# Emitting five engine streams straight into the main program, without a Block around them

## The chip, the cores and the metric

One core of one Trainium2 chip. The metric is the device time of one execution in microseconds (us).

The *span* is what the profile shows, from the start of the first instruction to the end of the last one of this program. The *time* is the metric; it is longer than the span (245.03 against 243.30 us in the profiled run of the kernel before). *Time minus span*: 1.73 us, though no instruction of the kernel lies in it. A store *lands*, as the word is used here, at the last count that the trace records for the semaphore of its transfer, a counter that an engine's instruction can wait for.

## The reference

A diffusion transformer block on x of 2 x 256 x 1152 in bf16, weights in bf16:

```python
B, N, D, F, H = 2, 256, 1152, 4608, 2
shift_a, scale_a, gate_a, shift_m, scale_m, gate_m = (silu(c) @ w_mod).reshape(B, 6, 1, D)   # split on axis 1
h = layernorm(x) * (1 + scale_a) + shift_a
q, k, v = h @ wqkv                                    # two heads of 576
a = softmax(q k^T * 576**-0.5) v @ wo
x = x + gate_a * a
h2 = layernorm(x) * (1 + scale_m) + shift_m
return x + gate_m * (gelu(h2 @ w_fc1) @ w_fc2)
```

## The kernel before

The kernel keeps a list of operations for each of the five engines (PE, ACT, DVE, POOL and SP, which issues 71 of the 79 transfers). A scheduler in Python works out their order and the semaphore waits. `emit` then writes each list into the program. Only `emit` and the line that opens the Block are touched by the change.

```python
outs = [ins for u in order["sp"] for ins in u.instrs if ins.is_out]     # 14 stores of the result
last_out = outs[-1]

def run_engine(e, eng_handle):
    for u in order[e]:
        for ins in u.instrs:
            if ins is last_out:                       # wait for all stores but the last four
                for o in outs[:-4]:
                    eng_handle.wait_ge(dma_sems[o.dma_sem], o.dma_val)
            for (k, v) in waits[ins.gidx]:
                # ... wait_ge on a DMA's semaphore or on an engine's
            bi = ins.fn(eng_handle)
            # ... bi.then_inc(...)
    if e == "sp":                                     # SP waits until the result is stored
        for o in outs[-4:-1]:
            eng_handle.wait_ge(dma_sems[o.dma_sem], o.dma_val)
        eng_handle.wait_ge(dma_sems[last_out.dma_sem], last_out.dma_val)

block.sync(lambda eng: run_engine("sp", eng))
block.tensor(lambda eng: run_engine("pe", eng))
# ... scalar, vector, gpsimd the same

# in build_kernel:
with (
    nc.sbuf_tensor("arena", ...) as arena,
    nc.psum_tensor("psum", ...) as psum,
    nc.Block() as block,                              # line 554
):
```

A Block gives each engine a body of its own. The author expected of it a branch into each body, a branch from the body to the Block's end, and a barrier of all engines there. Of the branches, the trace shows SP's at the end alone (38 ns at 242.919 us). The barrier is in the trace: the DRAINs of SP, ACT, DVE and PE count one semaphore (96) up; POOL's wait for it starts at 243.121 us, 25 ns after the last of them, SP's, has ended; POOL counts a second one (97) up at 243.199, and the waits of the other four for it start at 243.240 to 243.253. SP alone waits for the stores to land. The others have nothing to do after their last operation.

Of the kernel before, what the change touches and what calls it, by code (L numbers as in the profile page):

```python
# [171 lines left out]
class Sched:  # L172
# [222 lines left out]
        for e in ENGINES:  # L395
            print(e, "%.1f" % (sum(u.end - u.start for u in self.order[e]) / 1000))

    def emit(self, nc, block, sems, dma_sems):
        order = self.order
        eidx = {e: 0 for e in ENGINES}  # L400
        dma_cnt = [0] * len(dma_sems)
        n_other = getattr(self, "n_other_dma_sems", 8)
        n_sp = len(dma_sems) - n_other
        di = 0
        dj = 0
        for e in ENGINES:
            for u in order[e]:
                for ins in u.instrs:
                    if u.dma_bytes > 0:
                        if e == "sp":  # L410
                            k = di % n_sp
                            di += 1
                        else:
                            k = n_sp + dj % n_other
                            dj += 1
                        dma_cnt[k] += 16
                        ins.dma_sem = k
                        ins.dma_val = dma_cnt[k]
                    else:
                        eidx[e] += 1  # L420
                        ins.eidx = eidx[e]
        self.final_counts = dict(eidx)
        self.final_dma = list(dma_cnt)
        snap = {}
        stats = {"waits": 0}

        def sem_of(d):
            if d.dma_sem is not None:
                return ("d", d.dma_sem), d.dma_val
            return ("e", d.unit.eng), d.eidx  # L430

        allu = sorted(self.units, key=lambda u: (u.start, u.uid))
        known = {e: {} for e in ENGINES}
        waits = {}
        for u in allu:
            e = u.eng
            kn = known[e]
            for ins in u.instrs:
                need = {}
                for d in ins.deps:  # L440
                    k, v = sem_of(d)
                    if need.get(k, 0) < v:
                        need[k] = v
                wl = []
                for k, v in sorted(need.items(), key=lambda kv: (-kv[1], str(kv[0]))):
                    if kn.get(k, 0) >= v:
                        continue
                    wl.append((k, v))
                    kn[k] = v
                    for d in ins.deps:  # L450
                        if sem_of(d) == (k, v):
                            sn = snap.get(d.gidx)
                            if sn:
                                for kk, vv in sn.items():
                                    if kn.get(kk, 0) < vv:
                                        kn[kk] = vv
                            break
                waits[ins.gidx] = wl
                stats["waits"] += len(wl)
                snap[ins.gidx] = dict(kn)  # L460
        self.wait_stats = stats

        outs = [ins for u in order["sp"] for ins in u.instrs if ins.is_out]
# [5 lines that stand above are left out]
                    if ins is last_out:  # L469
# [3 lines that stand above are left out]
                        if k[0] == "d":  # L473
                            eng_handle.wait_ge(dma_sems[k[1]], v)
                        else:
                            eng_handle.wait_ge(sems[k[1]], v)  # L476
                    bi = ins.fn(eng_handle)
                    if ins.dma_sem is not None:
                        bi.then_inc(dma_sems[ins.dma_sem], 16)
                    else:  # L480
                        bi.then_inc(sems[e], 1)
            if e == "sp":
                for o in outs[-4:-1]:
                    eng_handle.wait_ge(dma_sems[o.dma_sem], o.dma_val)
                eng_handle.wait_ge(dma_sems[last_out.dma_sem], last_out.dma_val)

        block.sync(lambda eng: run_engine("sp", eng))
        block.tensor(lambda eng: run_engine("pe", eng))
        block.scalar(lambda eng: run_engine("act", eng))
        block.vector(lambda eng: run_engine("dve", eng))  # L490
        block.gpsimd(lambda eng: run_engine("pool", eng))



# [50 lines left out]
def build_kernel(nc, x, c, wqkv, wo, w_mod, w_fc1, w_fc2, out):  # L545
    S = Sched()
# [4 lines left out]
    with (  # L551
        nc.sbuf_tensor("arena", [P, ARENA_BYTES // 2], BF16) as arena,
        nc.psum_tensor("psum", [P, 4096], F32) as psum,
        nc.Block() as block,
    ):
        def sb(off, nbytes, dt=BF16):
            assert off % 4 == 0 and off + nbytes <= ARENA_BYTES, (off, nbytes)
# [741 lines left out]
        with ExitStack() as es:  # L1299
            sems = {e: es.enter_context(nc.semaphore("c_" + e)) for e in ENGINES}  # L1300
            dma_sems = [es.enter_context(nc.semaphore("d%d" % i)) for i in range(56)]
            S.emit(nc, block, sems, dma_sems)
    return S


# [3 lines left out]
def bass_standalone__dit_block__diffusion_kernel(  # L1309
    nc: bass.Bass,  # L1310
    x: bass.AP,
    c: bass.AP,
    wqkv: bass.AP,
    wo: bass.AP,
    w_mod: bass.AP,
    w_fc1: bass.AP,
    w_fc2: bass.AP,
    out: bass.AP,
):
    build_kernel(nc, x, c, wqkv, wo, w_mod, w_fc1, w_fc2, out)  # L1320
# [28 lines left out]
```

## Time and profile before

| | before |
|---|---|
| time, median of 6 runs (range) | 245.33 us (245.23 to 245.52) |
| time / span of the profiled run | 245.03 / 243.30 us |
| PE busy | 238.9 us, 98% of the span |
| last matmul ends / last store landed / last instruction ends | 240.59 / 242.81 / 243.30 us |

These lines of the page of the kernel before give the span, the engines' busy time, the granted clock in 40 slices (9 is 90% or more), and the shares of the chain of work that ended last.

```profile
span 243.3 us, 4087 instructions
...
PE 238.9 (98%) x1763; PEld 148.1 (61%) x1763; DVE 120.4 (49%) x217; ACT 67.2 (28%) x136; POOL 21.4 (9%) x39
...
PEclk9999999999999999999999999999999999999999
...
PE 94%; ACT 2%; DMA 2%; DVE 1%; POOL 0%; issue 0%; DVEq 0%
```

The kernel is bound by its matmuls (PE is 94% of the chain). A change that does not touch them can only win at the ends. The end of the chain in order of time (start us, us, what), kernel before:

```profile
105.90 134.88 PE psum L692 x848
240.78 0.02 issue
240.80 0.24 DVE arena L1272
241.04 0.02 issue
241.06 0.22 DVE arena L1273
```

The chain of work ends at 241.28 us, but the span ends at 243.3. The two microseconds in between hold no work of an engine: they are the last store on its way and then the closing of the Block. The instructions of line 554, the `with` that holds the Block, show the latter (engine, operation, count: durations in ns, first and last start in us; the letter q marks instructions of the engine's sequencer, which the page does not count as busy time):

```profile
L554 POOLq EVENT_SEMAPHORE  x2: 17/17/17, 243.1 to 243.2; - x2
L554 POOLq DRAIN  x1: 4317/4317/4317, 162.8 to 162.8; - x1
L554 ACTq DRAIN  x1: 626/626/626, 170.2 to 170.2; - x1
L554 PEldq DRAIN  x1: 897/897/897, 239.9 to 239.9; - x1
L554 DVEq DRAIN  x1: 261/261/261, 241.1 to 241.1; - x1
L554 SPq COMPARE_BRANCH  x1: 38/38/38, 242.9 to 242.9; - x1
L554 SPq DRAIN  x1: 7/7/7, 243.1 to 243.1; - x1
L554 SPq EVENT_SEMAPHORE  x1: 17/17/17, 243.2 to 243.2; - x1
L554 ACTq EVENT_SEMAPHORE  x1: 17/17/17, 243.2 to 243.2; - x1
L554 DVEq EVENT_SEMAPHORE  x1: 21/21/21, 243.3 to 243.3; - x1
L554 PEldq EVENT_SEMAPHORE  x1: 51/51/51, 243.3 to 243.3; - x1
```

Read it by the starts. The four DRAINs at 162.8 to 241.1 us come before the last store has landed (242.81), so they cost nothing, not even POOL's of 4.3 us. SP's branch, SP's DRAIN and all the semaphore instructions come after it and are exposed.

The start of the kernel before, in order of time (start us, us, engine, line, operation, out<-in, count):

```profile
0.80 0.84 SPq L673 DMA_DIRECT2D arena<-in_x_dram  x2
...
1.42 1.28 ACT L730 ACT_TABLE_LOAD   x1 [1.42 <-PEq L1334]
```

### The profile page before, as it was taken

How to read it: one execution, taken by the hardware profiler on the slowest of the kernel's cores; microseconds unless marked ns; L12 is line 12 of the kernel's file. 1: busy time of each engine (PE TensorE's matmuls, PEld its weight loads, DVE VectorE, ACT ScalarE, POOL GpSimd, SP SyncE). 2: the span in 40 equal slices, each digit the busy share in tenths (PEclk: the TensorE clock that was granted, in tenths of full speed). 3: DMA queues.
4: the chain of work that ended last, by engine and by line, in shares of the span. 5: the costliest groups of instructions: out<-in, count | busy, mean ns of one | idle time of the engine just before them, and what ended most of it. 6: DMA issues, size and time to landing. Idle time of an engine off the chain costs nothing.

```text
span 243.3 us, 4087 instructions
## 1 busy us (share of the span) xinstructions
PE 238.9 (98%) x1763; PEld 148.1 (61%) x1763; DVE 120.4 (49%) x217; ACT 67.2 (28%) x136; POOL 21.4 (9%) x39
## 2 busy tenths in 40 slices
PE   7999999999999999999999999999999999999995
PEld 2698854556667666898444444444565666656575
DVE  3824378596997799789999500000022221111112
ACT  4830350345424207973233222223000000000000
POOL 1500000000021186400000000020000000000000
PEclk9999999999999999999999999999999999999999
DMA  7999999999995999989953498002000000000000
GB/s 233 332 379 393 390 390 391 396 414 405 392 354 183 341 396 392 392 268 394 316 160 84 150 320 310 0 21 80 0 16 19 16 16 19 16 16 22 29 16 19
DMA packets 30140, 51.59 MB, mean 212 GB/s; under 512 B 1703, under 2 KB 15787, under 8 KB 30123
## 3 DMA queue, kind: packets, MB, share of 16 engines
q1 hardware_dynamic: 29680, 50.14, 57.9%
q0 software_dynamic: 416, 1.19, 1.7%
q8 instruction: 14, 0.23, 0.4%
q14 instruction: 3, 0.02, 0.0%
q10 hardware_dynamic: 27, 0.00, 0.0%
HBM read 50.14 MB, written 1.19 MB: 211 GB/s over the span
## 4 chain that ended last, share of the span: by engine, by line
PE 94%; ACT 2%; DMA 2%; DVE 1%; POOL 0%; issue 0%; DVEq 0%
PE psum L692 93%; PE psum L695 2%; DMA arena<-in_x_dram 2%; ACT arena L753 1%; ACT arena L751 1%; DVE arena L764 0%; POOL arena L755 0%; DVE arena L1272 0%; DVE arena L1273 0%; DVE arena L754 0%; DVE arena L746 0%; DVEq L476 0%
## 5 line engine op out<-in xcount | busy, mean ns | idle before, releaser
L692 PE MATMUL psum<-arena 128*128 128x384 bf16 (+10 forms) x1674 | 235.7, 307 | 1.5 <-POOL arena L715 1.5
L692 PEld LDWEIGHTS psum<-arena 128*128 128x128 bf16 (+3 forms) x1674 | 142.9, 97 | 90.1 <-issue 4.5
L1067 DVE SCALAR_TENSOR_TENSOR arena<-arena 128x1152 f32<-128x1152 bf16 x32 | 44.7, 1414 | 0.6
L1272 DVE TENSOR_TENSOR arena<-psum,arena 128x384 f32<-128x384 f32 (+3 forms) x14 | 7.0, 501 | 68.0 <-PE psum L692 68.0
L1181 ACT ACTIVATE arena<-psum 128x512 bf16<-128x512 f32 (+1 forms) x44 | 22.4, 520 | 42.7 <-PE psum L692 42.7
L687 ACT ACTIVATE arena<-psum 128x512 bf16<-128x512 f32 (+6 forms) x37 | 19.6, 550 | 38.7 <-PE psum L692 37.0
L689 DVE CAST arena<-psum 128x512 bf16<-128x512 f32 (+3 forms) x13 | 8.2, 641 | 11.4 <-PE psum L692 11.3
L673 POOL DMA_DIRECT2D dit_scratch<-arena x3 | 1.8, 616 | 115.3 <-DVE arena L689 58.5
L1149 POOL TENSOR_TENSOR arena<-arena 128x384 f32<-128x384 f32 x12 | 10.9, 912 | 10.8 <-DVE arena L1148 9.4
L1094 DVE CAST arena<-psum 72x32 bf16<-72x32 f32 x1 | 0.2, 188 | 21.3 <-PE psum L692 21.3
L743 DVE BATCH_NORM_STATS2 arena<-arena 128x6 f32<-128x384 f32 (+1 forms) x18 | 9.6, 551 | 0.3
L1154 ACT ACTIVATE arena<-arena 128x1152 bf16<-128x1152 f32 x4 | 5.3, 1344 | 11.8 <-DVE arena L1153 11.8
L1273 DVE TENSOR_TENSOR arena<-arena 128x384 bf16<-128x384 f32 (+3 forms) x14 | 7.0, 501 | 0.5
L1148 DVE TENSOR_TENSOR arena<-psum,arena 128x384 f32<-128x384 f32 x12 | 6.5, 547 | 1.5 <-PE psum L692 1.4
L695 PE MATMUL psum<-arena 128*128 128x128 bf16 (+1 forms) x89 | 7.1, 219 | 0.2 <-DVE arena L764 0.2
L695 PEld LDWEIGHTS psum<-arena 128*128 128x128 bf16 (+1 forms) x89 | 5.8, 98 | 2.2 <-DMA arena<-in_c_dram 0.8
L1168 DVE TENSOR_SCALAR arena<-psum,arena 128x128 bf16<-128x128 bf16 x20 | 5.4, 334 | 1.9 <-PE psum L695 1.9
L1171 ACT ACTIVATE arena<-psum,arena 128x128 bf16<-128x128 bf16 x16 | 6.0, 456 | 1.0 <-PE psum L692 0.6
L1074 DVE TENSOR_REDUCE arena<-arena 128x36 f32<-128x1152 f32 x4 | 5.4, 1345 | 0.0
L1071 DVE STREAM_TRANSPOSE arena<-arena 128x1152 f32<-128x1152 f32 x4 | 5.4, 1362 | 0.0
L997 ACT ACTIVATE arena<-psum,arena 128x256 bf16<-128x256 f32 x8 | 3.7, 472 | 1.3 <-PE psum L692 0.9
L951 ACT ACTIVATE arena<-arena 128x256 bf16<-128x256 bf16 x6 | 2.6, 498 | 3.9 <-DVE arena L945 3.9
(48 smaller groups left out, 45.9 us busy)
## 6 DMA issues: line engine op xcount, KB each, us to landing
arena<-in_w_fc_dram SPq DMA_DIRECT2D x9, 1152.0 KB, 7.1
arena<-in_w_fc_dram SPq DMA_DIRECT2D x4, 2592.0 KB, 17.3
arena<-in_wqkv_dram SPq DMA_DIRECT2D x18, 288.0 KB, 10.4
arena<-in_w_mod_dram SPq DMA_DIRECT2D x3, 1728.0 KB, 20.3
arena<-in_w_mod_dram SPq DMA_DIRECT2D x3, 864.0 KB, 13.4
arena<-in_w_mod_dram SPq DMA_DIRECT2D x9, 288.0 KB, 10.7
arena<-in_wqkv_dram SPq DMA_DIRECT2D x1, 2592.0 KB, 16.7
arena<-in_wo_dram SPq DMA_DIRECT2D x1, 2592.0 KB, 24.4
```

What stands on the lines that cost most here:

```text
L687: act(c_act(n), lambda e: e.activation(out=dst, in_=src, func=ACTF.Copy), [src], [dst], name)
L689: dve(c_dve_psum16(n) if psum16 else c_dve_psum32(n), lambda e: e.tensor_copy(dst, src), [src], [dst], name)
L692: S.instr(lambda e: e.matmul(o, lhsT=l, rhs=r, start=st, stop=sp, **kw), reads=[l, r], writes=[o])
L695: S.instr(lambda e: e.transpose(o, i_, idn), reads=[i_, idn], writes=[o])
L743: dve(550, lambda e, s=s, o=o: e.bn_stats(out=o, in_=s), [s], [o], "bn_%s_%d" % (tag, ci))
L1067: dve(1270, lambda e, w=w, s=s, acc=acc: e.scalar_tensor_tensor(out=acc, in0=w, scalar=s, in1=acc, op0=ALU.mult, op1=ALU.add), [w, s, acc] ...
L1148: dve(550, lambda e, o=o, ga=ga, x1c=x1c: e.tensor_tensor(out=x1c, in0=o, in1=ga, op=ALU.mult), [o, ga], [x1c], "wo_t1_%d_%d" % (t, ci))
L1149: S.op("pool", 930, lambda e, xs=xs, x1c=x1c: e.tensor_tensor(out=x1c, in0=x1c, in1=xs, op=ALU.add), reads=[x1c, xs], writes=[x1c], name=" ...
L1171: act(440, lambda e, o=o, dst=dst, s1=s1, s2=s2: e.activation(out=dst, in_=o, func=ACTF.Identity, scale=s1, bias=s2), [o, s1, s2], [dst], ...
L1181: act(c_act(ntok), lambda e: e.activation(out=dst, in_=o, func=ACTF.Gelu_apprx_tanh), [o], [dst], "gelu_%d_%d" % (f, tok0))
L1272: dve(c_dve_psum32(w), lambda e, o=o, gm=gm, t1=t1: e.tensor_tensor(out=t1, in0=o, in1=gm, op=ALU.mult), [o, gm], [t1], "fc2_t1_%d_%d" % ( ...
L1273: dve(c_dve_32(w), lambda e, t1=t1, x1c=x1c, ost=ost: e.tensor_tensor(out=ost, in0=t1, in1=x1c, op=ALU.add), [t1, x1c], [ost], "fc2_out_%d ...
```

## The change

The intent is to save what the Block adds: the branches and the closing barrier. The same lists are written into the one main program, each instruction with its engine's handle.

```diff
-    def emit(self, nc, block, sems, dma_sems):
+    def emit(self, nc, sems, dma_sems):
 ...
-        block.sync(lambda eng: run_engine("sp", eng))
-        block.tensor(lambda eng: run_engine("pe", eng))
-        block.scalar(lambda eng: run_engine("act", eng))
-        block.vector(lambda eng: run_engine("dve", eng))
-        block.gpsimd(lambda eng: run_engine("pool", eng))
+        for e, eng in (("sp", nc.sync), ("pe", nc.tensor), ("act", nc.scalar), ("dve", nc.vector), ("pool", nc.gpsimd)):
+            run_engine(e, eng)
 ...
         nc.psum_tensor("psum", [P, 4096], F32) as psum,
-        nc.Block() as block,
     ):
 ...
-            S.emit(nc, block, sems, dma_sems)
+            S.emit(nc, sems, dma_sems)
```

## The prediction

> **What bounds the kernel now.** TensorE. The page's busy table gives PE 238.9 us of a 243.3 us span (98%), and the chain of waits is PE for 94%: from 11.3 to 240.8 us it is matmuls and transposes, with the granted clock at full in all 40 slices. What is not PE lies at the ends: 11.3 us before the first dependent transpose (loading x 3.96 us, layernorm statistics), and 2.5 us after the last matmul (two DVE operations of 0.24 and 0.22 us, the last 16 KB store, 1.4 us to landing, then the Block's end).
>
> **What the change removes, adds, moves.** Work per engine, order, semaphores and buffers stay: the same scheduler fills the same lists, only the emission differs. The Block stands for:
> 1. A branch into each engine's body. The instruction records show none executed: after the opening barrier (the library's own, it stays) SP is released at 0.71 us and issues its first DMA 83 ns later, as between another SP wait and its DMA (81 ns near the end). Nothing is won at the start.
> 2. A branch from each body to the Block's end. Only SP's is in the records (it carries the last store wait): 38 ns at 242.92 us; SP's next instruction, a DRAIN, starts at 243.09, 170 ns after the branch did.
> 3. The closing barrier (line of the `with`): SP DRAIN 243.09, POOL's semaphore instructions 243.12 and 243.20, release of the others 243.24 to 243.30. The other engines' DRAINs run earlier and are hidden (PE 239.9, DVE 241.1 us).
> Added: one plain wait on SP for the one that the branch carried.
>
> **How much is critical.** Items 2 and 3 come after the last store landed (242.81 us), so they are exposed: from about 242.94 to 243.30, 0.35 us. [...] After the span the runtime has its own barrier[...]. The profiled run's time (245.03) is 1.73 us above the span, so part of it may be counted. Four engines will now wait there before SP arrives, so it may shorten: one hop of it comes 213 ns after the one before, where the same hop takes 38 ns in the preamble; 0 to 0.25 us may be saved. The 239 us of matmuls are untouched.
>
> **Predicted time.** 245.29 - 0.35 - about 0.10 = 244.85 us (estimate), range 244.45 to 245.25. Faster by over 2%: 0.01; within 2%: 0.98; slower: 0.01. Repeats differ by 0.3 us, so it is just visible.
>
> **What would show each step.** Span 242.9 to 243.0 us. No DRAIN, branch or barrier semaphore after the last store wait; SP's wait is the last instruction. Start unchanged: first DMA about 80 ns after SP's release, dependent transposes at 11.3 us. PE busy within 0.3 us of 238.9, same matmul count. Time minus span 1.5 to 1.75 us.
>
> **What would make it wrong.** The library closing the main program with a barrier of its own (then no gain); other placing of waits or of the activation table load (1.28 us at 1.42 us on ACT, hidden now behind loading x) when all engines share one block; shifted instruction fetches starving PE (its 16 KB fetches take about 1.1 us each, hidden now); noise as large as the effect.

245.29 (median of the three runs known then) - 0.35 - 0.10 comes to 244.84, and the forecast says 244.85. The 0.35 us were read from the trace. The 0.10 us, and that a part of the 1.73 us above the span is the runtime's barrier, were estimates. What the trace of before shows beside them is two rows of nine counts of one semaphore, described below, and in them one step (from the second to the third) of 213 ns after the kernel and 38 ns ahead of it.

## More of the kernel before

All runs but one are fast ones (granted TensorE clock 0.998 to 1.000); the one slow run is named where it occurs and is used for no time.

PE is the engine that is released last (its semaphore instruction lasts 51 ns and ends the span).

The wait for the last store is the instruction ahead of the branch:

```profile
L485 SPq EVENT_SEMAPHORE  x1: 28/28/28, 242.8 to 242.8; - x1
```

In the trace it starts at 242.829 us, 16 ns after the landing. The branch (242.919 us) also carries a wait on a store, but on an older one, which had landed at 237.40 us; so the branch waits for nothing.

## The result, and the profile after

Ratios are the mean time of one kernel's fast runs over that of the other's fast runs of the same rounds, so not quite the ratio of the medians.

| | before | after |
|---|---|---|
| time, median of 6 runs (range) | 245.33 us (245.23 to 245.52) | 244.28 us (243.99 to 244.74) |
| ratio, 95% interval | | 0.9958 (0.9946 to 0.9971) |
| time / span of the profiled run | 245.03 / 243.30 us | 244.28 / 243.00 us |
| time minus span | 1.73 us | 1.28 us |
| last store landed | 242.81 us | 242.85 us |

The change is a win of about 1 us (0.4%). It is clear of the noise, and larger than predicted: 244.28 lies below the low end of the range, 244.45. The table already shows where to look: the span fell by 0.3 us, and time minus span by 0.45 us, though no instruction of the kernel lies there.

The page of the changed kernel, the same lines:

```profile
span 243.0 us, 4065 instructions
...
PE 238.2 (98%) x1753; PEld 148.0 (61%) x1763; DVE 120.4 (50%) x217; ACT 67.2 (28%) x136; POOL 21.5 (9%) x39
...
PE 94%; DMA 3%; SPq 1%; issue 0%; DVE 0%
```

The 22 instructions fewer are the Block's 12, and 10 matmuls whose records are missing from this trace (the weight loads are all there, 1763 of 1763, and so are the compiled matmuls). The chain's shares at the start differ because it is followed back through another of two inputs: in after through the transfer of w_mod, which ends at 10.75 us, in before through layernorm's DVE operation, which ends at 11.28 us (11.05 in after).

The start and the end of the changed kernel's run, in order of time; first the start:

```profile
0.79 0.84 SPq L669 DMA_DIRECT2D arena<-in_x_dram  x2
...
1.43 1.28 ACT L726 ACT_TABLE_LOAD   x1 [1.43 <-PEq L1330]
```

Nothing moved there: the records show no branch at the start of either kernel. The first dependent transposes came at 11.1 instead of 11.3 us, but by 14.3 us the two runs are level again. The end of its chain:

```profile
169.43 71.39 PE psum L688 x507
240.84 0.24 DVE arena L1268
241.07 0.02 issue
241.10 0.23 DVE arena L1269
```

The last piece of work starts 0.04 us later than before, so the matmuls gave nothing. Line 554's instructions are gone; the last instruction of the program is now SP's wait for the last store (line 485):

```profile
L485 SPq EVENT_SEMAPHORE  x1: 28/28/28, 243.0 to 243.0; - x1
```

What lies after the span can be seen from the trace's records of semaphore 2. No instruction of the kernel touches it and it stands on no page. It is taken here for the counter of a barrier of the runtime; that is inferred, since a row of nine counts, from -0.370 to 0.001 us in before, also leads up to the start of the span. All that follows about this barrier is read from these counts. Each count is called a mark here. The nine marks of the first barrier after the kernel's work, in us from the start of the span:

```
         1        2        3        4        5        6        7        8        9
before   243.542  243.576  243.789  243.832  243.855  243.953  243.991  244.027  244.074
after    240.978  241.012  241.050  241.472  243.168  243.212  243.250  243.284  243.331
```

Before, all nine come after the end of the span (243.304); they take 0.53 us, and mark 9 comes 0.77 us after the end. After, four of them come long before the last store has landed, the fifth 0.17 us after SP's last wait, and mark 9 only 0.33 us after the end of the span. Take that distance from time minus span, and the two kernels are alike: 0.96 and 0.95 us are left. (The same is left, 0.94 to 0.96 us, in nine of the twelve fast profiles; in e4, e7 and e10 it is 1.03 to 1.08 us, and no record says why.) So 0.30 us were saved in the span and 0.44 us in the runtime's barrier, together 0.74, against a difference of 0.75 us between the two profiled runs.

### The profile page after: what moved, and what is told of

The parts are those of the page before. It is cut to its first block, busy times and chain, and to the rows that moved or that the text cites. A ratio compares the mean times of both kernels' runs of the same rounds, so it can differ in the third digit from the quotient of the medians.

```text
span 243.0 us, 4065 instructions
## 1 busy us (share of the span) xinstructions
PE 238.2 (98%) x1753; PEld 148.0 (61%) x1763; DVE 120.4 (50%) x217; ACT 67.2 (28%) x136; POOL 21.5 (9%) x39
## 4 chain that ended last, share of the span: by engine, by line
PE 94%; DMA 3%; SPq 1%; issue 0%; DVE 0%
PE psum L688 93%; DMA arena<-in_w_mod_dram 3%; PE psum L691 1%; SPq L669 1%; DVE arena L805 0%; DVE arena L1268 0%; DVE arena L1269 0%
## 5 line engine op out<-in xcount | busy, mean ns | idle before, releaser
L688 PE MATMUL psum<-arena 128*128 128x384 bf16 (+12 forms) x1664 | 234.8, 307 | 2.4 <-POOL arena L711 1.5
L685 DVE CAST arena<-psum 128x512 bf16<-128x512 f32 (+3 forms) x13 | 8.2, 641 | 11.4 <-PE psum L688 11.3
L1150 ACT ACTIVATE arena<-arena 128x1152 bf16<-128x1152 f32 x4 | 5.3, 1344 | 11.1 <-DVE arena L1149 11.1
```

The lines of the kernel that those rows point to most:

```text
L685: dve(c_dve_psum16(n) if psum16 else c_dve_psum32(n), lambda e: e.tensor_copy(dst, src), [src], [dst], name)
L688: S.instr(lambda e: e.matmul(o, lhsT=l, rhs=r, start=st, stop=sp, **kw), reads=[l, r], writes=[o])
```

## The experiments

Theory A: the gain is the end alone, made of the closing barrier with SP's branch, and of the runtime's barrier, whose first part now runs while the last store is under way. Rival B: the gain comes from how the streams lie in the program (no branches, instructions fetched at other moments). Rival C: of the closing of the Block, it is one item, such as POOL's DRAIN. All runs were correct.

| run | what it is | median us | ratio to before (95%) | mean time minus span | mark 9 after the end of the span |
|---|---|---|---|---|---|
| after | the change | 244.28 | 0.9958 (0.9946 to 0.9971) | 1.31 us | 0.33 us |
| e1 | barrier put back, no Block | 245.24 | 0.9995 (0.998 to 1.001) | 1.75 | 0.78 |
| e2 | all wait for the last store | 244.81 | 0.9984 (0.997 to 0.9998) | 1.71 | 0.79 |
| e3 | PE waits too | 244.61 | 0.9969 (0.9954 to 0.9984) | 1.43 | 0.47 |
| e4 | DVE waits too | 244.59 | 0.9967 (0.9953 to 0.9981) | 1.35 | 0.39 |
| e8 | the change again | 244.18 | 0.9966 (0.9953 to 0.9978) | 1.32 | 0.31 |
| e5 | POOL waits too | 244.69 | 0.9987 (0.9974 to 0.9999) | 1.79 | 0.83 |
| e7 | all but POOL wait | 244.49 | 0.9974 (0.996 to 0.9987) | 1.43 | 0.41 |
| e6 | SP's waits in another order | 244.18 | 0.9963 (0.995 to 0.9977) | 1.32 | slow profile |
| e9 | e6 again | 244.16 | 0.9956 (0.9944 to 0.9969) | 1.24 | 0.28 |
| e10 | the change, third time | 244.22 | 0.9962 (0.9949 to 0.9974) | 1.37 | 0.31 |
| e11 | Block closed by semaphores only | 245.19 | 1.0003 (0.9989 to 1.0016) | 1.71 | 0.76 |

The runs e1 to e4 shared one chip and its 11 runs of before (median 245.41); e5 to e8 shared another with 9 (245.08), e9 to e11 a third set with 9 (245.20). Before's own mean time minus span was 1.72, 1.73 and 1.77 us there. The record gives the spans of single runs to 0.1 us only, so these means are good to a few hundredths of a microsecond.

### e1: the barrier put back, without a Block

```diff
             run_engine(e, eng)
+        nc.all_engine_barrier()
```

> The changed kernel with one all-engine barrier put back at the very end of the main program (same streams, no Block). Theory A (the gain is the closing barrier and what it does to the runtime's barrier after it): time back at 245.1 to 245.5 us, ratio to before 0.999 to 1.001, time minus span back at about 1.73 us. Rival B (the gain comes from how the streams lie in one program: branches gone, instructions fetched at other moments): time stays at about 244.3 us, ratio about 0.996, whatever the barrier costs on top (at most 0.3 us).

Measured: 245.24 us, ratio 0.9995, time minus span 1.75 us. The instructions of the added line in e1:

```profile
L489 POOLq EVENT_SEMAPHORE  x2: 17/17/17, 243.4 to 243.4; - x2
...
L489 SPq DRAIN  x1: 40/40/40, 243.3 to 243.3; - x1
L489 SPq EVENT_SEMAPHORE  x1: 17/17/17, 243.5 to 243.5; - x1
...
L489 PEldq EVENT_SEMAPHORE  x1: 51/51/51, 243.5 to 243.5; - x1
```

One line of barrier takes back the whole gain, although the streams are those of the changed kernel. Rival B is out as the main cause; a share of up to 0.5 us is left to it by the interval of this timing. The traces leave it nothing ahead of the last store: the last DVE operation ends at 241.29 us in before, and at 241.32, 241.33 and 241.27 us in after, e8 and e10. The run also separates the branch from the barrier: from the start of SP's last wait on the stores to the end of the span it takes 338 ns here and 475 ns in before, where the branch stands in between. So the branch, with the 132 ns until the instruction after it, costs about 0.14 us, the barrier about 0.3. The timing alone (ratio 0.9995, so -0.12 us, interval -0.5 to +0.25) cannot resolve the branch. In e1's profiled run there was luck in it, too: SP's last wait itself started 198 ns after the landing (16 in before), which by chance makes up for the branch that is gone; this late start is among the open points below.

### e2: no barrier, but all five engines arrive together

```diff
             run_engine(e, eng)
+        for e in ("pe", "act", "dve", "pool"):
+            {"pe": nc.tensor, "act": nc.scalar, "dve": nc.vector, "pool": nc.gpsimd}[e].wait_ge(dma_sems[last_out.dma_sem], last_out.dma_val)
```

> The changed kernel, no barrier, but each of the other four engines ends its stream with a wait on the last store's semaphore, so that all five reach the runtime's barrier together. Theory A with two terms: the closing barrier stays gone (span 242.9 to 243.1), but the early arrival of the four engines is lost: time minus span rises from 1.30 to about 1.7 us, time about 244.7 us, ratio about 0.9976. If the whole gain is the closing barrier by itself: time as the changed kernel, 244.3.

Measured: 244.81 us, span of the profiled run 243.05, time minus span 1.71 us. The four added waits cost the span almost nothing, since all end within 36 ns of SP's own:

```profile
L490 ACTq EVENT_SEMAPHORE  x1: 17/17/17, 243.0 to 243.0; - x1
L490 POOLq EVENT_SEMAPHORE  x1: 17/17/17, 243.0 to 243.0; - x1
L490 DVEq EVENT_SEMAPHORE  x1: 21/21/21, 243.0 to 243.0; - x1
L490 PEldq EVENT_SEMAPHORE  x1: 51/51/51, 243.0 to 243.0; - x1
```

And yet more than half of the gain is gone: 0.39 us is left (ratio 0.9984, where 0.9976 was expected), against 1.03 us in the first comparison and 0.93 us as the mean of three. What is gone lies after the span. The changed kernel was not run again beside e2, but its time minus span was 1.31 to 1.37 us in each of its three sets of runs. So the gain has two terms, and the second is the early arrival of the other engines in the runtime's barrier. It goes with the closing barrier only because that barrier holds them back.

### e3 and e4: one engine arrives late

The edit is that of e2 with `("pe",)` and with `("dve",)`.

> As e2, but only PE waits for the last store. If the runtime's barrier is a chain that starts with PE and ends with SP (in the changed kernel four arrivals come before SP's, the earliest near PE's last matmul), PE alone arriving late exposes the whole chain: time minus span about 1.7, the same as e2, time about 244.7 us. If only the number of late engines counts: between the changed kernel and e2, near 244.4.

> As e2, but only DVE waits for the last store. If DVE stands late in the runtime's chain (its arrival seems the fourth of five), the early part of the chain is still hidden: time minus span 1.3 to 1.45 us, time 244.3 to 244.45. If only the number of late engines counts: the same as e3.

Measured: e3 1.43 us of time minus span and 244.61 us, e4 1.35 us and 244.59 us. The marks:

```
         1        2        3        4        5        6        7        8        9
e3       243.083  243.117  243.155  243.200  243.223  243.320  243.360  243.394  243.440
e4       240.800  240.834  240.873  242.860  242.888  242.981  243.021  243.055  243.102
```

PE's added wait ends at 242.89 in e3, and there is no mark until 0.19 us after that. DVE's ends at 242.71 in e4; three marks are early and the fourth comes 0.15 us after it. So PE is the first in the chain and DVE the fourth, as supposed. e4's time minus span came out as expected (1.3 to 1.45 us), though its time of 244.59 us lies above the 244.3 to 244.45 us that were written down. And e3's number was wrong: with the whole chain exposed, 1.7 us was expected and 1.43 measured. The chain itself takes 0.36 us in e3, where it took 0.53 in before, 0.54 in e1 and 0.60 in e2. The difference is the step from mark 2 to mark 3: 38 ns in e3, but 213, 221 and 279 ns in before, e1 and e2. Something that is third in the chain was late in those three. This left a choice of theories, and the next two runs were made for it.

### e5 and e7: POOL alone, and all but POOL

The edit is that of e2 with `("pool",)` and with `("pe", "act", "dve")`.

> As e2, but only POOL waits for the last store. In before, e1 and e2 the third mark of the runtime's chain came 0.54 to 0.58 us after POOL's last instruction, 0.2 to 0.28 us late; with PE alone late (e3) it was not late. Theory A2 (POOL is the third in the chain and slow to enter it): two marks early near 241 us, the third about 0.55 us after POOL's wait, then the rest of the chain, 0.29 us; time minus span 1.70 to 1.80, time about 244.8 us, as e2 though one engine alone is late. Rival (no engine is special, late arrivals cost by number): as e3 and e4, time minus span about 1.4, 244.5 us.

> As e2, but PE, ACT and DVE wait for the last store and POOL does not. Theory A2: the chain runs without the late third mark, time minus span 1.40 to 1.50 as e3, time about 244.5 us. Rival (number of late engines): close to e2, 1.65 or more, 244.7 us.

Measured: e5 1.79 us of time minus span (244.69 us), e7 1.43 us (244.49 us).

```
         1        2        3        4        5        6        7        8        9
e5       240.956  240.990  243.412  243.456  243.479  243.577  243.616  243.650  243.697
e7       243.162  243.196  243.234  243.278  243.302  243.399  243.438  243.473  243.519
```

POOL's only added instruction in e5:

```profile
L490 POOLq EVENT_SEMAPHORE  x1: 17/17/17, 242.9 to 242.9; - x1
```

It ends at 242.868; the third mark follows 0.54 us later. One late engine, POOL, costs as much as all four late (e2), and three late engines without POOL cost as little as PE alone (e3). The order is thus shown for PE (first), POOL (third), DVE (fourth) and SP (fifth); ACT is second by exclusion. So are the entry times, from an engine's last instruction to its mark: POOL 0.54 to 0.58 us (before, e1, e2, e5, e11), PE 0.19 to 0.24 where it ends with a wait (0.36 after its last matmul, whose end is modelled, in the other six fast profiles), DVE 0.15 and SP 0.12 to 0.18. What POOL does in its half microsecond no record shows.

### e8 and e10: the change again, beside more runs of before

> The changed kernel once more, beside many runs of the kernel before on one chip. Theory A (0.35 us of closing barrier plus 0.44 us of the runtime's barrier, nothing else): ratio 0.9968 (-0.79 us), mean span 0.35 us under that of before, time minus span 1.30 against 1.73 us. If something else gains too (the first comparison gave -1.0 us): ratio 0.9958, and the span 0.6 us shorter.

> The changed kernel a third time, as the partner of e9 and for a third comparison with before. Theory A: ratio to before 0.9966 to 0.9970, mean span 0.35 to 0.42 us shorter than before, time minus span 1.25 to 1.40 against 1.73 us.

Measured: e8 0.9966 with a mean span of 242.96 against 243.38 us, so 0.42 us of span and 0.41 us after it. e10 0.9962 with 242.94 against 243.52, so 0.58 and 0.40 us; a span shorter by 0.35 to 0.42 us was expected. The three ratios of the changed kernel average 0.9962, or 0.93 us. The 0.79 us that were expected lie within each of the three intervals, but every measured value is above them. The traces of e8 and e10 show why: their span ends 44 and 45 ns after the last landing, against 491 ns in before. That is 0.45 us, and not the 0.30 to 0.35 us of the first profile of after, whose last wait started 118 ns late (see the closing list). With 0.46 us for the runtime's barrier (mark 9 after the end of the span: 0.77 in before, 0.31 in e8 and e10) the traces explain 0.91 us.

### e6 and e9: SP's waits in another order

An attempt to beat the changed kernel. In it, two more small gaps stand at the end: SP waits for DVE in a semaphore instruction of its own ahead of the last store (in after the store is issued 108 ns after DVE's last operation ends), and its last wait sometimes starts late (118 ns after the landing in after).

```diff
-                    if ins is last_out:
-                        for o in outs[:-4]:
-                            eng_handle.wait_ge(dma_sems[o.dma_sem], o.dma_val)
                     for (k, v) in waits[ins.gidx]:
 ...
+                    if ins is last_out:
+                        for o in outs[:-3]:
+                            eng_handle.wait_ge(dma_sems[o.dma_sem], o.dma_val)
 ...
-                for o in outs[-4:-1]:
+                for o in (last_out, outs[-3], outs[-2]):
                     eng_handle.wait_ge(dma_sems[o.dma_sem], o.dma_val)
-                eng_handle.wait_ge(dma_sems[last_out.dma_sem], last_out.dma_val)
```

> An attempt to beat the changed kernel: same waits on SP in another order, so that the last store carries the wait on DVE itself (no semaphore instruction between DVE's last result and it) and the waits on the last two stores share SP's last instruction. In the changed kernel the last store is issued 108 ns after DVE's last operation ends (241.32 to 241.43) and SP's last wait starts 118 ns after the last landing, 445 ns after the wait before it. Expected: issue about 30 ns after DVE's end, last wait 17 ns after the landing, so 0.08 + 0.10 us less in the trace; time about 244.15 us, which the timing alone may not resolve from the changed kernel.

> e6 once more, since its profile fell in a slow run. In the trace: the last store is issued about 28 ns after DVE's end (108 to 109 in the changed kernel), SP's last instruction ends about 20 ns after the last landing (44 to 146). Time about 0.1 us under the changed kernel of the same chip (e10), which is within the noise of either.

Measured: e6's profiled run was slow (312.76 us at a granted clock of 0.756), its four other runs were fast; e9's were all fast. e6's clock has no known cause: nothing in the program differs from e9. In e9 the store is issued 28 ns after DVE's last operation ends (108 in the changed kernel), and the last wait ends 23 ns after the last landing. Both gaps closed as intended. The times are 244.22 (e6, mean of the fast runs) against 244.28 (e8), and 244.18 (e9) against 244.31 (e10): 0.06 and 0.13 us better, where 0.1 was expected. The runs of either kernel differ among themselves by 0.2 to 0.4 us, so by the timing this is not shown to be faster; only the trace shows the two gaps gone.

### e11: the Block kept, closed by semaphores only

```diff
-        nc.Block() as block,
+        nc.Block(no_gpsimd_drain=True) as block,
```

> The kernel before with the Block kept, but closed by semaphores alone (no DRAIN of POOL's queue). POOL's DRAIN of 4.3 us lies at 163 us, 80 us before the end, and is hidden. Theory A: nothing is won, since SP still gathers all engines after the last store and releases them together: time minus span 1.73, span and time as before or up to 0.1 us longer (one semaphore instruction more per engine), ratio 0.999 to 1.001. Rival (POOL's drain is what the Block costs): about 0.997, as the changed kernel.

Measured: 245.19 us, ratio 1.0003, time minus span 1.71. In e11 POOL's DRAIN is gone (the other four engines keep theirs), and what is exposed is still there:

```profile
L554 PEldq EVENT_SEMAPHORE  x2: 51/51/51, 240.6 to 243.0; - x2
...
L554 POOLq EVENT_SEMAPHORE  x2: 17/17/17, 242.9 to 243.0; - x2
...
L554 SPq COMPARE_BRANCH  x1: 38/38/38, 242.6 to 242.6; - x1
L554 SPq DRAIN  x1: 7/7/7, 242.8 to 242.8; - x1
```

Rival C, in the form of POOL's 4.3 us DRAIN, is out. The longest item of the barrier was worth nothing, because it ran 80 us before the end.

## Why the prediction was right or wrong

- *PE bounds the kernel and the matmuls are untouched*: right. The last DVE pieces start at 240.80 and 240.84 us, and e1 with the changed streams is as slow as before within its interval.
- *Nothing is won at the start*: right. The first transfer is issued at 0.80 and 0.79 us. At the start no branch stands in the records. After the only one, SP's at the end of before, the next instruction follows within 132 ns, with no instruction fetch in the DMA records in between (the nearest fetches start at 239.91 and 243.53 us).
- *The closing barrier and SP's branch are exposed, 0.35 us*: right in kind, a little small. It was counted from about 242.94 us, inside SP's branch, since the branch was thought to carry "the last store wait". As shown above, that wait was the instruction before it, and the branch waited for nothing; so no wait had to be added in its place, and the branch's whole place in the row of waits was saved. Measured from the last landing to the end of the span, it is 0.49 us before and 0.04 to 0.15 us after, so 0.35 to 0.45 us.
- *The library might add a barrier of its own, place waits otherwise or fetch worse*: it did nothing of this but regroup SP's last waits: before, they are three instructions, and the third is the branch; after, they are two plain waits of two semaphores each. The traces of before and after have 14 instruction fetches of 16 KB each within the span, of 0.93 to 1.35 us and of 0.88 to 1.25 us.
- *The runtime's barrier may shorten by 0 to 0.25 us, about 0.10*: this is the step that failed. The mechanism was right (four engines now wait there before SP arrives), and the size was off. In the prediction's words, "one hop of it comes 213 ns after the one before", and only that hop was taken as what can be saved. The runs show that everything ahead of SP's mark is hidden: PE's entry (0.24 us), POOL's late mark and the steps in between. What is left exposed is SP's own entry (0.14 to 0.17 us in after, e8 and e10) and the chain from mark 5 to mark 9 (0.16 us). Mark 9 came 0.77 us after the span before and 0.31 to 0.33 us after it now, a saving of 0.44 to 0.46 us. Time minus span, foretold as 1.5 to 1.75 us, came out at 1.31. The numbers for a better estimate were at hand in the trace of before: the nine marks ahead of the kernel take 371 ns, those after it 532 ns, and the last comes 0.77 us after the span (e3 later showed the chain with 357 ns). To see how much of it would be hidden needed one question more: which engine is first in the chain, and which engine was released last. It is PE in both.
- *The noise*: the term that was missed, about 0.35 us, is as large as the spread of repeats that the prediction had named (0.3 us). Only the means of several runs on one chip settle it.

What stays open: what POOL does for half a microsecond before it joins the runtime's barrier, the late start of SP's last wait described below, and the 0.1 us more after mark 9 in three of the profiles. ACT's place in the chain is known by exclusion only.

## What to carry to other kernels

At the end of this program, an all-engine barrier cost more than its own instructions (about 0.3 us): it made every engine reach the runtime's barrier late and together, so that all of that barrier was exposed behind the last store (0.44 to 0.46 us more). Where a kernel ends the same way, let the engines run out as soon as their work is done and let one engine, the one that comes last in the runtime's chain (here SP, mark 5), wait for the result to land; above all do not hold POOL, which by itself cost as much here as all four (time minus span 1.79 us in e5, 1.71 in e2). Compare time minus span and not only spans: about half of this gain lies where the profile of the kernel shows no instruction.

## Further measurements

- The nine marks are unevenly spaced: 34, 38, 45, 23, 97, 40, 34 and 46 ns from one to the next in e3.
- In the nine fast profiles with the changed kernel's order of waits, SP's last wait never started sooner than 436 ns after the start of the wait before it. In after, e1, e3 and e7 it started 436 to 445 ns after that and 118 to 198 ns after the last landing; where the waits lay further apart (592 to 692 ns in e5, e8 and e10, 472 ns in e2, and 608 ns in before with its other order) it started 16 or 17 ns after the last landing. e4 lies at the edge, with 441 and 18 ns. The cause is open.
- One run, the profiled one of e6, took 312.76 us at a mean granted clock of 0.756, with a program that is the same as e9's, whose profiled run took 243.97 us. The trace has the clock at 0.752 from 4.8 us on for the next 307 us. Its cause is open too.
